# DeltaNet and Fourier mix: a fourth buffer for keys, outputs as pairs of tiles, and the second group's inversion between the steps of the chain

## The chip, the core and the metric

The kernel runs on one NeuronCore of one Trainium2 chip. The metric is the device time of one execution in microseconds (us). The engines are named as the profile names them: PE (TensorE, matmuls), DVE (VectorE), ACT (ScalarE), POOL (GpSimd) and SP (SyncE, which issues DMA transfers here). Each engine works through a list of instructions in a fixed order; an instruction that waits holds up all that stand behind it on its engine.

## What is computed

The inputs q, k, v and beta are float32; the two weight matrices come as 64-bit words, which the kernel turns into float32. The first part is DeltaNet, a recurrence over 768 time steps for 4 batches and 8 heads of dimension 48; the second mixes the result by a real two-dimensional Fourier transform, normalises the rows, and applies a two-layer network.

```python
k_n = k / (np.linalg.norm(k, axis=-1, keepdims=True) + 1e-06)
for t in range(S):                                   # S = 768
    y[:, :, t] = q[t] @ state
    state = state + beta[t] * outer(k_n[t], v[t] - k_n[t] @ state)
x = y as (4, 768, 384)
u = x + real(fft(fft(x, axis=1), axis=2))
un = (u - mean(u)) / sqrt(var(u) + 1e-06)            # over the last axis
out = u + relu(un @ w_ch1) @ w_ch2                   # 384 -> 1536 -> 384
```

## The kernel before, in words

**Chunks, quads, groups.** Time is cut into chunks of 64 steps, 12 for each batch. All 8 heads of a chunk are worked on together. Four chunks make a quad Q (12 in all, three for each batch), two quads a group g (6 in all). The chain runs over the 48 chunks m = 0 to 47, one after the other, because each needs the state that the last one left; chunks 12, 24 and 36 begin a new batch and so a new state.

**Ahead of the chain**, for each quad, `prepare` (L343) transposes keys and queries on PE (tiles `pt`), copies them to the tile `KQT` on ACT (L383 to L388), multiplies keys by keys and by queries (`pg`), copies the products of keys to a triangular system `A` (L414 on DVE, L416 on ACT) and masks those with the queries into `LQ` on DVE (L419). Called for keys alone or queries alone, it does half of this: `keys` and `queries` (L828, L834) do so for the first four quads.

For each group, `invert` (L451) solves the triangular systems of two quads on DVE: a transpose of `A` into `X` (L457), the norms (L428 to L449), a loop of 30 turns with a product (L472) and a sum (L474) each, a product into `Y` (L477), and two transposes into `Z` (L481) and back to `A` (L483). The same function then puts each quad's two 32-wide halves together, in two steps of matmuls (`pj`, L501) and four copies on ACT each (L505 to L509), into the tile `wt`. The second group's `A` lies in `w2`, the space that the second layer's weights fill later; the turns write their products back into `A`.

**A chain step** `chain(m)` (L534): the product of keys and state (`pc<-st`), a difference on DVE (L569, `U` in the first batch and `R` later), in later batches one more product with `wt` (`pc<-R,wt`) and a copy on ACT (L582), the product for the new state (`pc<-U,kp`), and the sum into the other state tile (L599). `outputs` (L605) adds the step's output into `py`, and ACT copies it (L619). In the first batch, `combined` (L514) folds `wt` into keys and values beforehand (`pm`, `pv`). `scaled` (L190) multiplies a quad's values by the lengths of its keys on DVE (L195).

**Beside the chain** go the weights and the second part of the reference. `weights` (L255) loads 64-bit words in slots and turns each piece of 384 columns to float32 by two instructions on ACT (L295, L297) and three on DVE (L311, L314, L317); part 0 is the first layer's `w1`, part 1 is `w2`, with three slots that lie in an output buffer. `fourier(b)` (L646) makes sums and differences of a batch's tiles (L660 and below, tile `scr`), multiplies them with tables (`pf`, `pb`) and adds the result (L696); `mlp` (L733) normalises (`un`, L742), transposes, and runs the two layers (`ph`, `po`).

**What sets the order.** The driver at the end (L839 to L893) steps through generators. At each yield of a chain step it advances `pre` (the preparation and inversion of the group to come) by 2.4 steps and, from step 8 on, `side` (weights, Fourier, network) by 2.4 steps too; before step 8 `side` gets only what `pre` has left over. This gives the program order. A scheduler then places each engine's instructions, with the buffers' releases as limits; what `tc.keep_in_program_order` encloses stays behind all that was traced before it on its engine. `NB` counts the buffers of `KQT`, `LQ` and `wt`.

Of the kernel before, what the change touches and what calls it, by code (L numbers as in the profile page):

```python
# [17 lines left out]
CH = 64  # L18
# [64 lines left out]
def kernel(  # L83
# [23 lines left out]
    NB = 3  # L107
# [15 lines left out]
    def mm(o, lhsT, rhs, start, stop=True):  # L123
        nc.tensor.matmul(o, lhsT=lhsT, rhs=rhs, start=start, stop=stop, skip_group_check=True)  # L124
# [24 lines left out]

    kps = [zeroed([128, QT, 4, 64], f"kp{i}", nc.vector, pads) for i in range(NB + 1)]  # L150
    qps = [zeroed([128, QT, 4, 64], f"qp{i}", nc.vector, pads) for i in range(2)]
    wts = [zeroed([128, QT, 4, CH], f"wt{i}", nc.gpsimd) for i in range(NB)]
# [93 lines left out]
    xbufs = [const.tile([128, NC, DM], F32, name=f"x{i}") for i in range(3)]  # L246
# [8 lines left out]
    def weights(part):  # L255
# [14 lines left out]
        if part == 0:  # L270
            halves = [(w1v[:, i, a * nw:a * nw + nw], w1[:, i, a * nw:a * nw + nw])
                      for i in range(KD) for a in range(2)]
            n, stage = 2, wk.tile([128, 2, nw, 2], I32, tag="hT", name="w64")
        else:
            halves = [(w2v[:, i, a * np_:a * np_ + np_], w2[:, i, a * np_:a * np_ + np_])
                      for i in range(KF) for a in range(DM // np_)]
            n, stage = 1, xbufs[2].rearrange("p t d -> p (t d)")[:, 0:6 * np_].bitcast(I32).rearrange(
                "p (i f two) -> p i f two", i=3, two=2)
        ns = stage.shape[1]

        def fetched(i):
            if i < len(halves):
                nc.sync.dma_start(out=stage[:, i % ns], in_=halves[i][0])

        def words(p):
            i, cs = p // n % ns, slice(p % n * np_, (p % n + 1) * np_)
            return stage[:, i, cs, 0], stage[:, i, cs, 1], tmps[p % 2]
# [12 lines left out]
        for i in range(ns):  # L300
            fetched(i)
        yield
        tmps = [wk.tile([128, 2, np_], I32, tag=tag, name="wtmp") for tag in ("F", "scr")]
        first(0)
        for p in range(n * len(halves)):
# [13 lines left out]
            if (p + 1) % n == 0:  # L319
                fetched(p // n + ns)  # L320
# [8 lines left out]
    def squares(Q):  # L329
# [5 lines left out]
        if Q < 4:  # L335
            Ksq = xbufs[1].rearrange("p t d -> p (t d)")[:, Q % 2 * QT * 4 * D:(Q % 2 + 1) * QT * 4 * D]
            Ksq = Ksq.rearrange("p (n d) -> p n d", d=D)
        else:
            Ksq = wk.tile([128, QT * 4, D], F32, tag="Y", name="Ksq")
# [3 lines left out]
    def prepare(Q, parts=(0, 1)):  # L343
# [5 lines left out]
        again = Q == NB and parts == (1,)  # L349
        taken = (0, 1) if again else parts  # L350
        g, lh = divmod(Q, 2)
        if 0 in parts:
# [7 lines left out]
            if Q == NB:  # L360
                KQT = w2.rearrange("p c m -> p (c m)")[:, 2048:2048 + QT * 8 * CH].rearrange(
                    "p (c j h a t) -> p c j h a t", c=QT, j=2, h=2, a=2)
        if Q != NB and 0 in parts or again:
            KQT = wk.tile([128, QT, 2, 2, 2, CH], F32, tag="KQT", bufs=NB, name="KQT")
        if 0 in parts or again:
# [5 lines left out]
        for c2 in range(QT // 2):  # L371
            for c in (2 * c2, 2 * c2 + 1):
                nt, at0 = len(taken), taken[0]
                pt = ps_one([128, nt, 2, 2, CH], "pt")
                for a in taken:
                    for j in range(2):
                        tr(pt[:, a - at0, j].rearrange("p h t -> p (h t)"),
                           (kp, qp)[a][:, c, 2 * j:2 * j + 2, :].rearrange("p u d -> p (u d)"),
                           a == at0 and j == 0)
                dst = KQT[:, c, :, :, at0:at0 + nt].rearrange("p j h a t -> p a (j h) t")  # L380
# [3 lines left out]
                else:  # L384

                    if nt == 2:
                        nc.scalar.activation(dst[:, 0], src[:, 0], ACT.Copy)
                    nc.scalar.activation(dst[:, nt - 1], src[:, nt - 1, :, ::-1], ACT.Copy)  # L388
# [62 lines left out]
    def invert(g):  # L451
# [3 lines left out]
        A = grams.pop(g)  # L455
        X = wk.tile([128, W, W], F32, tag="X", name="X")
        nc.vector.transpose(X.rearrange("p s t -> p (s t)"),  # L457
                            A[:, :, :, 0].rearrange("p c u s -> p s (c u)"))
# [10 lines left out]
        for j in range(1, W - 1):  # L469
            n = W - 1 - j  # L470
            t = A.rearrange("p c u sl s -> p (c u) sl s")[:, 0:j, 0, 0:n]
            nc.vector.tensor_tensor(t, X[:, j:j + 1, j + 1:].broadcast_to([128, j, n]),  # L472
                                    X[:, 0:j, j:j + 1].broadcast_to([128, j, n]), op=ALU.mult)
# [450 lines left out]
```

## Time and profile before

| | us |
|---|---|
| median of 14 runs | 828.78 |
| lowest and highest of them | 820.47, 840.18 |
| the profiled execution, its time | 831.21 |
| its span, first to last instruction | 829.5 |

The profile has one execution. Its page gives busy times of each engine, the span cut in 40 slices, and groups of instructions. Its other views are a timeline of one engine (start, duration, engine, line, operation, output<-inputs, and in brackets how long the engine had been idle and what ended that), a table of busy times by stretches of the span, groups of instructions within a stretch, and waits added up by what was waited for. Most fp32 matmuls leave more than one record, so counts in the trace are above those of the program. The lines that count are quoted in the prediction.

### The profile page before, as it was taken

The numbers are of one execution on the slowest core, as the hardware profiler recorded it, in microseconds if no ns is written. First come the engines' busy times: TensorE is split into PE (matmuls) and PEld (weight loads), VectorE is DVE, ScalarE is ACT, GpSimd is POOL, SyncE is SP. The second block draws the span as 40 slices with busy tenths as digits, with TensorE's granted clock in tenths as the row PEclk, the third lists the DMA queues.
The fourth block names the chain that finished last, engine by engine and source line by source line (L and its number), as shares of the span: only waits on it lengthen the run. The fifth ranks groups of instructions, "written<-read, shape, count | busy, mean of one in ns | idle before, by whom it ended". The sixth has DMA issues, their size and how long they took to land.

```text
span 829.5 us, 19211 instructions
## 1 busy us (share of the span) xinstructions
PE 738.0 (89%) x8224; PEld 549.5 (66%) x8224; DVE 396.7 (48%) x1036; ACT 290.0 (35%) x679; POOL 45.7 (6%) x67
## 2 busy tenths in 40 slices
PE   3637958996989997889999999999899989999997
PEld 3426857775758765665766766766667667676784
DVE  5885868559964137981169313499110125210000
ACT  3826348253545142371431632511521113030120
POOL 3000000101000000010000001000000010000000
PEclk9999966596997997999999699999699999999999
DMA  7442225212510121101101001001000000000000
GB/s 154 102 111 70 47 40 157 48 29 66 135 40 12 29 49 26 20 13 36 32 17 44 3 10 30 2 1 39 2 6 15 1 20 1 10 9 20 10 9 20
DMA packets 84149, 30.84 MB, mean 37 GB/s; under 512 B 79344, under 2 KB 80880, under 8 KB 84064
## 3 DMA queue, kind: packets, MB, share of 16 engines
q1 hardware_dynamic: 80976, 26.63, 14.4%
q0 software_dynamic: 912, 2.59, 0.9%
q8 instruction: 65, 1.06, 0.5%
q10 hardware_dynamic: 2176, 0.39, 0.3%
q14 instruction: 20, 0.16, 0.1%
HBM read 24.87 MB, written 4.72 MB: 36 GB/s over the span
## 4 chain that ended last, share of the span: by engine, by line
PE 68%; DVE 13%; ACT 11%; DMA 3%; issue 3%; SPq 1%; POOL 0%; POOLq 0%; ACTq 0%; DVEq 0%
PE po L124 20%; PE ph L124 20%; PE py L124 6%; PE pc L124 5%; PE pg L124 3%; PE pj L124 3%; PE pf L124 3%; DVE X L474 2%; PE pt L127 2%; DVE A L472 2%; PE pb L124 2%; ACT wt L506 2%; ACT A L416 2%; DMA x<-in_moe_w_ch_dram 1%; ACT wt L509 1%
## 5 line engine op out<-in xcount | busy, mean ns | idle before, releaser
L124 PE MATMUL ph<-unT,w 128*128 128x256 f32 x864 | 222.6, 405 | 6.2 <-ACT hT L759 2.9
L124 PE MATMUL po<-w,hT 128*128 128x384 f32 x576 | 199.2, 494 | 0.0
L124 PEld LDWEIGHTS ph<-unT,w 128*128 128x128 f32 x864 | 163.0, 198 | 37.1 <-ACT hT L759 6.2
L124 PEld LDWEIGHTS po<-w,hT 128*128 128x128 f32 x576 | 105.3, 190 | 65.8 <-issue 0.3
L759 ACT ACTIVATE hT<-ph 128x256 f32<-128x256 f32 x144 | 54.8, 384 | 185.8 <-PE ph L124 185.4
L599 DVE TENSOR_TENSOR st<-st,pc 48x192 f32<-48x192 f32 x88 | 30.8, 350 | 88.6 <-PE pc L124 62.2
L772 DVE TENSOR_TENSOR x<-x,po 128x384 f32<-128x384 f32 x24 | 13.3, 554 | 120.2 <-PE po L124 120.1
L472 DVE TENSOR_TENSOR A<-X 128x30 f32<-128x30 f32 (+9 forms) x150 | 50.3, 335 | 3.5
L124 PE MATMUL py<-st,KQT 128*64 128x96 f32 x384 | 49.8, 278 | 2.2 <-ACT x L619 2.1
L474 DVE TENSOR_TENSOR X<-X,A 128x30 f32<-128x30 f32 (+9 forms) x150 | 49.4, 329 | 3.4
L582 ACT ACTIVATE U<-pc 128x192 f32<-128x192 f32 x36 | 11.9, 331 | 111.5 <-PE pc L124 96.5
L124 PE MATMUL pg<-KQT 48*64 48x128 f32 (+1 forms) x960 | 36.7, 302 | 13.7 <-ACT KQT L383 13.0
L124 PEld LDWEIGHTS py<-st,KQT 128*64 128x64 f32 x384 | 38.4, 153 | 9.4 <-ACT x L619 4.1
L416 ACT ACTIVATE A<-pg 32x256 f32<-32x256 f32 x108 | 36.7, 369 | 20.4 <-PE pg L124 18.3
L124 PEld LDWEIGHTS pg<-KQT 48*64 48x64 f32 x960 | 29.1, 175 | 21.9 <-ACT KQT L383 16.3
L124 PE MATMUL py<-U,LQ 64*64 64x48 f32 x768 | 42.8, 240 | 0.0
L124 PEld LDWEIGHTS pc<-R,wt 64*64 64x64 f32 x576 | 23.4, 145 | 23.8 <-issue 8.8
L124 PE MATMUL pc<-R,wt 64*64 64x48 f32 x576 | 29.5, 235 | 10.7 <-DVE R L569 6.7
L124 PEld LDWEIGHTS py<-U,LQ 64*64 64x64 f32 x768 | 35.6, 152 | 3.9 <-issue 2.7
L696 DVE TENSOR_TENSOR x<-x,pb 128x193 f32<-128x193 f32 (+1 forms) x96 | 27.1, 344 | 18.4 <-PE pb L124 18.3
L639 POOL DMA_INDIRECT out_dram<-x,rows_hi x12 | 12.2, 1013 | 414.7 <-DVE x L772 198.2
L124 PE MATMUL pf<-stab,scr 128*128 128x128 f32 (+6 forms) x192 | 27.4, 292 | 8.5 <-DVE scr L670 8.3
(133 smaller groups left out, 860.4 us busy)
## 6 DMA issues: line engine op xcount, KB each, us to landing
w<-in_moe_w_ch_dram SPq DMA_DIRECT2D x6, 768.0 KB, 5.0
qp<-in_q_dram SPq DMA_DIRECT2D x96, 48.0 KB, 2.4
V<-in_v_dram SPq DMA_DIRECT2D x96, 48.0 KB, 2.4
x<-in_moe_w_ch_dram SPq DMA_DIRECT2D x12, 384.0 KB, 3.6
kp<-in_k_dram SPq DMA_DIRECT2D x88, 48.0 KB, 2.4
out_dram<-x SPq DMA_DIRECT2D x8, 192.0 KB, 1.9
out_dram<-x SPq DMA_DIRECT2D x4, 168.0 KB, 2.1
stab<-k_stab SPq DMA_DIRECT2D x1, 640.5 KB
```

Source lines behind the costliest of these rows:

```text
L124: nc.tensor.matmul(o, lhsT=lhsT, rhs=rhs, start=start, stop=stop, skip_group_check=True)
L127: nc.tensor.matmul(o, lhsT=src, rhs=ident[0:src.shape[0], 0:src.shape[0]], is_transpose=True, start=start, stop=True, skip_group_check=True)
L416: nc.scalar.activation(ce(A[pr, ns, :, sl]), src, ACT.Copy)
L472: nc.vector.tensor_tensor(t, X[:, j:j + 1, j + 1:].broadcast_to([128, j, n]), X[:, 0:j, j:j + 1].broadcast_to([128, j, n]), op=ALU.mult)
L474: nc.vector.tensor_tensor(X[:, 0:j, j + 1:], X[:, 0:j, j + 1:], t, op=ALU.add)
L506: nc.scalar.activation(wt[r1, :, :, 0:W], Z[r1, ns], ACT.Copy)
L582: nc.scalar.activation(U, pu, ACT.Copy)
L599: nc.vector.tensor_tensor(nst[pr, :, :, e, :], st[pr, :, :, e, :], pS[pr], op=ALU.add)
L639: nc.gpsimd.indirect_dma_start(out=out.rearrange("b s m -> (b s) m"), out_offset=bass.IndirectOffsetOnAxis(ap=rows_hi[:, i:i + 1], axis=0) ...
L696: nc.vector.tensor_tensor(dst, dst, src, op=op)
L759: nc.scalar.activation(hT[:, fc, :], ph, ACT.Relu)
L772: nc.vector.tensor_tensor(x[:, T, :], x[:, T, :], po, op=ALU.add)
```

## The change

- `NB` is 4 for `KQT` and `LQ`; `wt` keeps three buffers (`NW`). There were four buffers for loaded keys and there still are; loaded queries have one buffer instead of two. The fourth quad's keys, which had been transposed into space of `w2` and transposed once more later, go straight to the fourth `KQT`: 8 transposes on PE are gone.
- The three output buffers of six tiles become seven tiles of two, one for each pair that the Fourier mix joins (`xpairs`, `OF_BATCH`).
- `weights(0)` starts after the first loads of keys, queries and values. None of its pieces stands ahead of the first inversion any longer. `w2` is loaded through two slots instead of three (one pair tile and a tile under the tag `scr`).
- For the first two quads, 4 of 6 copies into `A` are on DVE, where 3 of 6 were.
- `invert` ends with the transposes; the rest is `merge`. For the first group, `merge` is called for the first quad alone ahead of the chain and for the second quad within it. The second group's `X` lies in `w2`, and its loop is held in program order. The first matmul of each `pj` is held in program order too.
- Group 2's inversion is not started before `fourier(0)` has been put into the program, and `fourier(0)` is put there as a whole.
- In `fourier`, one sum of 128x1152 (L660) becomes three of 128x384, and its second stage writes to the tile `F`.

```diff
-    NB = 3
+    NB, NW = 4, 3
-    qps = [... for i in range(2)]
-    wts = [... for i in range(NB)]
+    qps = [... for i in range(1)]
+    wts = [... for i in range(NW)]
-    xbufs = [const.tile([128, NC, DM], F32, name=f"x{i}") for i in range(3)]
+    xpairs = [const.tile([128, 2, DM], F32, name=f"x{i}") for i in range(2 * TH + 1)]
+    OF_BATCH = [(0, 1, 2), (3, 4, 5), (0, 1, 6), (3, 4, 2)]
...
-            n, stage = 1, xbufs[2]...   # three slots
+            n, stages = 1, [xpairs[6]...]
+        if part == 1:
+            stages.append(wk.tile([128, np_, 2], I32, tag="scr", name="w64"))
+            fetched(1)
-                fetched(p // n + ns)
+                fetched(p // n + 2)
...
-        again = Q == NB and parts == (1,)
-            if Q == NB:
-                KQT = w2...[:, 2048:2048 + QT * 8 * CH]...
-                        if Q < 2 and hh:
+                        if Q < 2 and (hh or sl):
                             nc.vector.tensor_copy(ce(A[pr, ns, :, sl]), src)
...
     def invert(g):
+        pin = tc.keep_in_program_order if g == 1 else lambda ins: ins
+        if g == 1:
+            X = w2...[:, 2048:2048 + W * W]
+        else:
             X = wk.tile([128, W, W], F32, tag="X", name="X")
-            nc.vector.tensor_tensor(t, ...)
-            nc.vector.tensor_tensor(X[:, 0:j, j + 1:], ...)
+            pin(nc.vector.tensor_tensor(t, ...))
+            pin(nc.vector.tensor_tensor(X[:, 0:j, j + 1:], ...))
...
-        for lh in range(2):
+    def merge(g, lhs=(0, 1)):
+        for lh in lhs:
-                            mm(pj[r1, hh, c, u], *ops, c == 0 and u == 0)
+                            ins = mm(pj[r1, hh, c, u], *ops, c == 0 and u == 0)
+                            if n % QT == 0 and u == 0 and hh == 0:
+                                tc.keep_in_program_order(ins)
...
     def ahead(g):
+        while g == 2 and 0 not in mixed:
+            yield
         yield from invert(g)
+        yield from merge(g)
...
-            yield from fourier(b)
+            run(fourier(b))
+            mixed.add(b)
+            yield
...
-    side = weights(0)
-    advance(side)
-    advance(side, 4)
-    load(1, 1)
+    side = weights(0)
+    advance(side)
     run(both(first, seq(keys(2, 3), queries(0, 1))))
+    pre = both(invert(1), queries(2, 3))
+    advance(pre, 2)
+    run(merge(0, (0,)))
     combined(0)
     combined(1)
-    pre = both(invert(1), queries(2, 3))
+    pre = seq(merge(0, (1,)), pre, merge(1))
```

The scheduler's lists show how this moves instructions. On DVE, between the first inversion's end and the second's loop, stood before (`w_114` is the space of `w2`, `V_978` the values of the second quad):

```order
L481 STREAM_TRANSPOSE Z<-Y 128x32x32
L483 STREAM_TRANSPOSE A<-Y 128x32x32
L195 TENSOR_TENSOR V_978<-V_978,ln 128x768
L457 STREAM_TRANSPOSE X<-w_114 128x1024
L462 SCALAR_TENSOR_TENSOR X<-X,bl 128x1024
L472 TENSOR_TENSOR w_114<-X 128x30
L474 TENSOR_TENSOR X<-X,w_114 128x30
```

and now, with the lines of the changed kernel (L575 is the step's difference, L605 the sum into the state, L414 is `LQ`):

```order
L195 TENSOR_TENSOR V_957<-V_957,ln 128x768
L481 STREAM_TRANSPOSE Z<-Y 128x32x32
L483 STREAM_TRANSPOSE A<-Y 128x32x32
L457 STREAM_TRANSPOSE w_112<-w_112 128x1024
L462 SCALAR_TENSOR_TENSOR w_112<-w_112,bl 128x1024
L476 MEMSET w_112 128x32
L562 COPY st_88<-p_820 48x4x48 x2
L575 TENSOR_TENSOR U<-V_321,pc 128x2x2x48
L605 TENSOR_TENSOR st_90<-st_88,pc 48x4x48 x2
L575 TENSOR_TENSOR U<-V_321,pc 128x2x2x48
L414 TENSOR_TENSOR LQ<-pg,pack 128x2x4x64
L472 TENSOR_TENSOR w_112<-w_112 128x30
```

The loop's first turn now stands behind the differences of steps 0 and 1 and behind the third quad's first `LQ`. On PE, from the first group's merges to the first chain step, stood before:

```order
L124 MATMUL pj<-Z,A 32x32 x32
L124 MATMUL pj<-A 32x32 x32
L124 MATMUL pv<-V_337,wt_84 64x48 x2
L124 MATMUL pj<-Z,A 32x32 x32
L124 MATMUL pv<-V_337,wt_84 64x48 x14
L124 MATMUL pj<-A 32x32 x32
L124 MATMUL p_887<-v0m,k_66 48x192 x2
L127 MATMUL pt<-pack,qp_80 128x128 x2
L124 MATMUL pm<-wt_84,kp_72 64x64 x8
L127 MATMUL pt<-pack,qp_80 128x128 x2
L124 MATMUL pv<-V_337,wt_84 64x48 x5
L124 MATMUL pm<-wt_84,kp_72 64x64 x8
```

and now stands, up to the first `LQ`'s matmuls, with pieces of steps 0 and 1 between:

```order
L124 MATMUL pc<-st_88,KQT 64x48 x8
L124 MATMUL pj<-Z,A 32x32 x32
L127 MATMUL pt<-pack,qp_80 128x128 x2
L124 MATMUL pc<-U,kp_72 48x48 x8
L127 MATMUL pt<-pack,qp_80 128x128 x2
L124 MATMUL py<-st_88,KQT 64x96 x2
L124 MATMUL pj<-A 32x32 x32
L127 MATMUL pt<-pack,qp_80 128x128 x2
L124 MATMUL pc<-st_90,KQT 64x48 x8
```

The first quad's two `pj`, 24 `pv`, 16 `pm` and `p` stand ahead of these rows; the second quad's merge has gone behind step 0, and 16 `pg` for `LQ` follow behind step 1. On DVE, the fourth group's inversion (g = 3) began before like this:

```order
L569 TENSOR_TENSOR R<-V_2913,pc 128x2x2x48
L772 TENSOR_TENSOR x_131<-x_131,po 128x384
L419 TENSOR_TENSOR LQ<-pg,pack 128x2x4x64
L599 TENSOR_TENSOR st_90<-st_92,pc 48x4x48 x2
L457 STREAM_TRANSPOSE X<-A 128x1024
L419 TENSOR_TENSOR LQ<-pg,pack 128x2x4x64
L462 SCALAR_TENSOR_TENSOR X<-X,bl 128x1024
```

and begins now like this:

```order
L575 TENSOR_TENSOR R<-V_2342,pc 128x2x2x48
L414 TENSOR_TENSOR LQ<-pg,pack 128x2x4x64
L605 TENSOR_TENSOR st_88<-st_90,pc 48x4x48 x2
L457 STREAM_TRANSPOSE X<-A 128x1024
L414 TENSOR_TENSOR LQ<-pg,pack 128x2x4x64
L575 TENSOR_TENSOR R<-V_2342,pc 128x2x2x48
L462 SCALAR_TENSOR_TENSOR X<-X,bl 128x1024
```

The transpose stood behind the difference of step 21 and stands behind that of step 17 now, so that the loop falls into the network's stretch and not into the next Fourier mix. In the same way PE's lists put the merges of groups 3, 4 and 5 just before steps 23, 31 and 39, where they stood behind steps 24, 32 and 40.

More of the change, by code (lines that the diff above doesn't have):

```diff
@@ L273, in weights @@
             n, stage = 2, wk.tile([128, 2, nw, 2], I32, tag="hT", name="w64")
+            stages = [stage[:, i] for i in range(2)]
         else:
@@ L298, in first @@
                 t[:, 1].bitcast(F32), hi.bitcast(F32), ACT.Abs, scale=2.0 ** -112))
-        for i in range(ns):
+        for i in range(len(stages)):
             fetched(i)
         yield
-        tmps = [wk.tile([128, 2, np_], I32, tag=tag, name="wtmp") for tag in ("F", "scr")]
+        if part == 1:
+            stages.append(wk.tile([128, np_, 2], I32, tag="scr", name="w64"))
+            fetched(1)
+        tmps = wk.tile([128, 2, 2, np_], I32, tag="F", name="wtmp")
         first(0)
@@ L372, in prepare @@
             for c in (2 * c2, 2 * c2 + 1):
[L373 to L375 removed]
+                pt = ps_one([128, na, 2, 2, CH], "pt")
+                for a in parts:
                     for j in range(2):
[L377 removed]
+                        tr(pt[:, a - a0, j].rearrange("p h t -> p (h t)"),
                            (kp, qp)[a][:, c, 2 * j:2 * j + 2, :].rearrange("p u d -> p (u d)"),
[L379 to L380 removed]
+                           a == a0 and j == 0)
+                dst = KQT[:, c, :, :, a0:a0 + na].rearrange("p j h a t -> p a (j h) t")
                 src = pt.rearrange("p a j h t -> p a (j h) t")
```

102 lines of the change are left out of this document (49 added, 53 removed).

## The prediction

> **What bounds the kernel now.** I read the page first, then busy times by stretches of the span, then the timelines of DVE and PE at the stretches' borders. The page:
>
> ```profile
> span 829.5 us, 19211 instructions
> PE 738.0 (89%) x8224; PEld 549.5 (66%) x8224; DVE 396.7 (48%) x1036; ACT 290.0 (35%) x679; POOL 45.7 (6%) x67
> ```
>
> PE is busy for 89% of the span. Little can be gained where it is full; what the change can move is where PE is not full or runs at a low clock. The stretches (start and end, length, then busy us and records of PE, PEld, DVE, ACT, POOL, the clock granted, the DMA share and GB/s):
>
> ```profile
> core 0: us, PE busy (x) PEld busy (x) DVE busy (x) ACT busy (x) POOL busy (x), PEclk, DMA share, GB/s
> 80.00:116.00 36.00, 29.52 (x702) 25.26 (x700) 30.68 (x84) 10.45 (x26) 0.00 (x0) 0.93 0.30 54
> 116.00:139.00 23.00, 20.22 (x483) 18.40 (x484) 13.69 (x28) 20.13 (x41) 0.00 (x0) 0.52 0.43 124
> 139.00:160.00 21.00, 18.77 (x324) 15.12 (x321) 12.58 (x35) 10.32 (x29) 1.27 (x1) 0.64 0.28 50
> 160.00:197.00 37.00, 29.17 (x322) 23.02 (x321) 26.38 (x73) 12.18 (x32) 4.17 (x8) 0.78 0.15 27
> 197.00:241.00 44.00, 42.87 (x272) 30.61 (x272) 40.06 (x109) 20.66 (x48) 0.73 (x1) 0.93 0.42 108
> 252.00:308.00 56.00, 56.00 (x727) 41.26 (x721) 14.78 (x38) 20.43 (x55) 2.28 (x2) 0.92 0.17 33
> 308.00:372.00 64.00, 51.51 (x741) 40.74 (x740) 54.20 (x151) 27.18 (x60) 4.91 (x7) 0.92 0.10 18
> 372.00:600.00 228.00, 219.31 (x2391) 158.00 (x2384) 110.15 (x280) 77.87 (x183) 10.70 (x15) 0.94 0.09 20
> ...
> 308.00:330.00 22.00, 14.83 (x170) 11.94 (x170) 18.74 (x48) 3.48 (x9) 1.62 (x2) 0.77 0.13 24
> ```
>
> Two stretches matter. From 80 to 116 the second group's inversion runs on DVE (30.68 of 36 us) and step 7 waits for it; from 308 to 372 the second Fourier mix and the fourth group's inversion share DVE (54.20 of 64), and PE is idle for 12.5 us. Between them, from 252 to 308, DVE has 14.78 us of work in 56 while PE is full.
>
> **The change, part by part.** Sums go against the profiled execution (831.21 us, 2.4 above the median of 828.78); the difference is then applied to the median.
>
> *The chain's start.* PE's rows (start, duration) before, around the first two steps:
>
> ```profile
> 71.20 1.92 PE L124 MATMUL pj<-Z,A 32*32 32x32 f32 x64
> 74.91 1.92 PE L124 MATMUL pj<-A 32*32 32x32 f32 x64
> 77.56 0.69 PE L127 MATMUL pt<-pack,qp 128*128 128x128 f32 x2
> 80.39 0.32 PE L124 MATMUL pc<-st,KQT 48*64 48x48 f32 x3
> 85.56 1.13 PE L124 MATMUL pg<-KQT 48*64 48x64 f32 x32
> 86.47 0.62 PE L124 MATMUL pc<-st,KQT 48*64 48x48 f32 x16
> ```
>
> The second quad's two `pj`, 3.8 us, leave the way of step 0, and so do 4 `pt` (two take 0.69): step 0 starts at some 75.3 instead of 80.4. That gains nothing by itself, because step 7 stands behind the second group's merges in both orders. The conversions, `X` and 128x768 value scaling around the first `Z` shift by a microsecond each way; I count nothing there.
>
> *The second inversion starts later.* DVE's rows:
>
> ```profile
> 61.58 2.02 DVE L481 STREAM_TRANSPOSE Z<-Y 128x1024 f32<-128x1024 f32 x1
> 76.46 0.19 DVE L472 TENSOR_TENSOR w<-X 128x30 f32<-128x30 f32 x1
> 86.76 0.69 DVE L419 TENSOR_TENSOR LQ<-pg,pack 128x512 f32<-128x512 f32 x1 [0.56 <-PE pg L124]
> 113.97 1.98 DVE L481 STREAM_TRANSPOSE Z<-Y 128x1024 f32<-128x1024 f32 x1
> 127.69 0.35 DVE L569 TENSOR_TENSOR U<-V,pc 128x192 f32<-128x192 f32 x1
> 158.47 0.35 DVE L569 TENSOR_TENSOR R<-V,pc 128x192 f32<-128x192 f32 x1 [1.95 <-PE pc L124]
> 165.63 0.35 DVE L569 TENSOR_TENSOR R<-V,pc 128x192 f32<-128x192 f32 x1
> ```
>
> The first turn ran at 76.46, at once behind `X`. Now step 1's difference and the third quad's first `LQ` stand ahead of it, and that `LQ` waits on PE for step 1. Steps 0 to 1 took 6.1 us (80.39 to 86.47); with the two `pj` between them and two times 32 records of `pg` (1.13 each; I take 2.1) out, step 1 is at 75.3 + 6.1 + 3.8 - 2.1 = 83.1, and its `pm`, `pv` and the 16 `pg` put `LQ`'s end near 87.4. From the first turn to the `Z` it took 37.5 us; a weight piece (1.5), a copy, two differences, a state sum, an `LQ` and two waits for `pg` (together 4.7) are no longer inside, so `Z` starts near 87.4 + 37.5 - 6.2 = 118.7 and ends near 120.7, 4.7 us later than at 115.95. Without the wait it would have ended earlier, so the added wait is behind PE's step 1: what is queued behind it on DVE is the whole loop.
>
> *Steps 7 to 12.* One `pj` of 1.9 us less stands ahead of step 7, so its difference moves by about 1.5 to 3 us. Then ACT decides:
>
> ```profile
> L295 ACT ACTIVATE wtmp<-w 128x384 int32<-128x384 uint32 x9 | 5.0, 554 | 0.0
> L416 ACT ACTIVATE A<-pg 32x256 f32<-32x256 f32 x12 | 4.1, 369 | 2.5 <-PE pg L124 2.4
> ```
>
> From 116 to 160 ACT had 20.13 + 10.32 = 30.5 us of work, 9 of the 12 conversions of the first layer and one quad's copies among it. All 12 are now there (3 more, at 2 x 0.55 each: 3.3), and the sixth quad's preparation too: at least the 4.1 us of its copies into `A`, at most the 12.18 us of ACT in the stretch 160 to 197; I take 8. That makes 41.8 us behind a `Z` at 120.7, so step 12 (158.47 before) comes no earlier than 162.5. Were all of it added in full, it would come at 158.5 + 4.7 + 11.3 = 174.5. I take 168, in the middle: ACT was idle for 14 of 44 us, and some of that idleness is filled.
>
> *The first Fourier mix.* It took from 160 to 197. The third group's `X` (1.9), its scaling (1.2) and an `LQ` (0.69) leave DVE's queue there; with 26.38 of 37 us busy I count 2.5 of these 3.8. So the network starts at 168 + 36 = 204 where it started at 197: **+7**, from +5 to +9.
>
> *The third group's inversion*, beside the second layer's weights, ended at 240.8:
>
> ```profile
> 206.89 0.55 DVE L311 SCALAR_TENSOR_TENSOR wtmp<-x,wtmp 128x384 int32<-128x384 int32 x1
> 207.36 0.35 DVE L314 TENSOR_SCALAR wtmp<-wtmp 128x384 int32<-128x384 int32 x1
> 207.87 0.55 DVE L317 CUSTOM_DVE_ANT_0 w<-wtmp 128x768 uint16<-128x768 uint16 x1
> 212.45 0.55 DVE L311 SCALAR_TENSOR_TENSOR wtmp<-x,wtmp 128x384 int32<-128x384 int32 x1
> 238.86 1.97 DVE L481 STREAM_TRANSPOSE Z<-Y 128x1024 f32<-128x1024 f32 x1
> ...
> x<-in_moe_w_ch_dram SPq DMA_DIRECT2D x12, 384.0 KB, 3.6
> ```
>
> The two rows of L311 are three pieces apart: 5.56 us is one turn of a slot, made of the load (3.6), two ACT instructions (1.1) and this one. With three slots a piece takes 1.85 us, with two 2.8. Twelve pieces then need 5 turns, 27.8 us, for 3 turns, 16.7. Not all of these 11 us count, since turns of the loop stand between the pieces in both orders: with two pieces at 1.45 (0.55, 0.35, 0.55) and some five loop instructions at 0.35 to 0.4, DVE has about 4.7 us of work in each 5.56. I get two ends: bound by DVE's work alone, and with four turns (2.3 us) done ahead, +7 - 2.3 = +4.7; bound by the loads, 206.5 + 27.8 + 3 for the last pieces + 9.7 for the rest of the loop, `Y` and `Z` = 247, +6.2. I take **+5.5**, from +2.7 (network at +5) to +8.2 (at +9).
>
> *Steps 17 to 24.* The fourth group's preparation and inversion now come early, into a full PE and an idle DVE. The network's work is used up earlier, and steps 20 to 23 have hardly any beside them. The nearest rows are those of steps 22 and 23 and what PE did between:
>
> ```profile
> 310.81 0.35 DVE L569 TENSOR_TENSOR R<-V,pc 128x192 f32<-128x192 f32 x1
> 316.18 0.35 DVE L569 TENSOR_TENSOR R<-V,pc 128x192 f32<-128x192 f32 x1 [1.22 <-PE pc L124]
> ...
> 311.81 0.69 PE L127 MATMUL ptr<-pack,un 128*128 128x128 f32 x3
> 313.78 1.96 PE L124 MATMUL ph<-unT,w 128*128 128x256 f32 x4
> ```
>
> The step took 5.37 us, 2.65 of it network work. Without that, three such steps leave 8 us of PE idle, less the two `pj` (3.8) that stand there now: **+4**. If the steps last as long as from 12 to 13 (7.16 us, rows above), it is 3 x 4.4 - 3.8 = +9.4; if `pj` and preparation cover all, 0.
>
> *The second Fourier mix.* DVE's largest group from 308 to 372 is half of the inversion's loop:
>
> ```profile
> L472 DVE TENSOR_TENSOR A<-X 128x30 f32<-128x30 f32 (+14 forms) x30 | 10.9, 364 | 0.5
> ```
>
> The other half (L474) is as many sums, so some 21 of the 54.20 us are the loop, and some 8 more its transposes and products. They go to where DVE was idle. PE's 12.5 us of idleness should then fall to what a mix without an inversion shows: from 372 to 600 PE is idle for 3.8% of the time, 2.5 us in 64; I leave 3, so 9.5 are gained, and 1.5 for the clock, which was 0.77 from 308 to 330 (at 14.83 us of PE work, 3.4 at most). **-11**; from -14 to -6, if only the first 22 us, 7.2 of them idle, lose 4.5 and 1.5.
>
> *The last two merges* stand a step earlier on PE; what they waited for from 372 to 600:
>
> ```profile
> PE pc L124 <- ACT wt L508: 3.2, 2, 2.0
> PE pj L124 <- DVE Z L481: 1.5, 2, 1.1
> ```
>
> At most 4.7 is saved, at least nothing: **-2**. The eight transposes less and three sums for one in `fourier` are below 1 us each way, beside full engines.
>
> **Sum:** +5.5 + 4 - 11 - 2 = -3.5 us. 831.2 becomes 827.7, and the median 828.8 becomes **825.3**.
>
> **The rivals.**
>
> *Full relief.* The fourth buffer takes the inversions out of PE's way and the starved steps are covered: +2.7 + 0 - 14 - 4.7 = -16, 812.8 us. For it: DVE's 14.78 of 56 us from 252 to 308. Against it: PE is full there, so that work taken in early pushes other work out.
>
> *No effect that can be told.* The second mix waits for its own sums, not for the inversion, and loses only 6 us of its idleness: 5.5 + 4 - 6 - 2 = +1.5, 830.3. For it: 7.2 of the 12.5 us lie in the first 22 us, where the mix makes its first sums.
>
> *Slower: steps 20 to 23 starve.* Each step is as long as its chain of waits over PE, DVE and ACT when nothing else is there. At 7.16 us a step, +9.4, and with a gain of only 6 behind it: 5.5 + 9.4 - 6 - 0 = +8.9, 837.7. It decides from about 6 us a step on. Against it: 5.37 us was seen with the clock low.
>
> *The clock.* From 116 to 139 PE is busy for 20.22 of 23 us, and the granted clock is 0.52. If the clock came back there, PE's 29.17 us of the first mix, at 0.78, could shrink by 3 to 6, and the time would be 822. The Trainium skill, in "TensorE: Matmul & The Clock Gate", Part 1, says that the full rate returns after about 3.4 us of sustained work. By that rule the 23 us at 0.52 could not be; the trace disagrees, so it has a small chance.
>
> **How the numbers follow.** Forecast 0.38 (821 to 830); relief 0.20; no effect 0.17; starving 0.20; clock 0.05. About 0.5% is what a measurement of this kernel can tell from no change: below 824.6 is faster, above 832.9 slower. Faster: 0.17 of the forecast, 0.20 and 0.04, 0.41. Same: 0.19, 0.12 and 0.01, 0.32. Slower: 0.02, 0.05 and 0.20, 0.27. The range has the bounds of the unknown terms, with relief and starving less 1 in 10 at either end: 811 to 840.
>
> **What would show it.** Right: the second loop's first turn near 87 and `Z` near 121; step 12 near 168; weight pieces of `w2` 2.8 us apart; the fourth group's turns between steps 18 and 22; PE idle near steps 21 to 23 and little in the second mix. Wrong: a turn of the loop ahead of the third quad's `LQ`; step 12 before 163; pieces 1.9 us apart; or PE idle for 10 us or more in the second mix, which would mean that DVE was not what it waited for.

## The result, and the profile after

The changed kernel takes 808.9 us (median of 10 runs, 805.6 to 814.5) against 829.4 us (47 runs): a ratio of 0.9787, with a 95% interval from 0.9754 to 0.982. The forecast was 825.3; its range from 811 to 840 holds 0.9787 x 828.78 = 811.1 only at its very edge, which is luck: the lower bound came from the terms of full relief, and those are not what made up the difference (see below). The change is some 2% faster, where I had expected hardly anything.

The pages' first lines, after the change, with the slices of the granted clock, which the prediction did not show for the kernel before:

```profile
span 805.0 us, 19238 instructions
PE 717.8 (89%) x8216; PEld 534.0 (66%) x8216; DVE 400.6 (50%) x1055; ACT 288.3 (36%) x675; POOL 47.5 (6%) x67
PEclk9999985879999998699999999999999999999999
```

and before:

```profile
PEclk9999966596997997999999699999699999999999
```

PE's share is 89% in both, but its busy time fell by 20.2 us, with 8 records less of 8224. A matmul that takes longer counts as busier, and the two low digits of the clock beyond slice 20 (6 in slices 23 and 29) are gone. What the clock does to a matmul shows in `pj` of the same 64 records, from two merges of the kernel before, the first at full clock and the second at half:

```profile
352.98 1.20 PE L124 MATMUL pj<-Z,A 32*32 32x32 f32 x64
462.89 1.92 PE L124 MATMUL pj<-Z,A 32*32 32x32 f32 x64 [0.17 <-ACT wt L508]
```

I cut both spans at the same two places of the program: the difference on DVE of step 24 and that of step 41. The columns are those of the prediction's table of stretches. After:

```profile
0.00:328.60 328.60, 255.99 (x4160) 199.03 (x4162) 231.09 (x597) 157.22 (x362) 21.13 (x31) 0.90 0.30 70
328.60:576.62 248.02, 243.05 (x2777) 178.38 (x2775) 134.09 (x361) 91.33 (x217) 16.03 (x22) 0.99 0.10 22
576.62:805.00 228.38, 218.73 (x1286) 156.61 (x1285) 35.41 (x98) 39.70 (x97) 10.31 (x14) 0.99 0.03 11
```

Before:

```profile
0.00:318.60 318.60, 257.39 (x3970) 201.23 (x3971) 206.37 (x538) 148.07 (x347) 19.79 (x31) 0.88 0.32 71
318.60:598.74 280.14, 261.06 (x2993) 191.25 (x2989) 155.43 (x406) 102.54 (x236) 15.61 (x22) 0.95 0.09 20
598.74:829.50 230.76, 219.53 (x1270) 157.03 (x1270) 34.94 (x94) 39.35 (x96) 10.31 (x14) 0.98 0.03 11
```

Step 24 comes 10.0 us later. From there to step 41 it is 32.1 us less, and behind it 2.4 less: 24.5 in all (these two executions lie a little further apart than the medians). In the middle stretch, idle time of PE fell from 19.1 to 5.0 us, and the clock rose from 0.95 to 0.99, which is 14.0 and 2.5 us of full clock lost. Some work moved out of this stretch to the first one: group 3's first three `pj`, which took 1.20 us each there, 3.6 in all, and nine records of `ph`, some 2.3 us:

```profile
L124 PE MATMUL ph<-unT,w 128*128 128x256 f32 x327 | 91.3, 417 | 4.1 <-ACT hT L759 2.0 <-ACT KQT L388 0.7 <-ACT gz L693 0.6
L124 PE MATMUL ph<-unT,w 128*128 128x256 f32 x318 | 80.2, 392 | 2.4 <-ACT hT L765 1.0 <-ACT KQT L383 0.9 <-ACT F L697 0.2
```

So 32.1 is 14.1 of idleness, some 11.5 of clock (a clock of two digits leaves 1 to 2 us open), 5.9 of moved work, and 0.6 that I did not take apart.

Cut further, at steps 27 and 36, the middle stretch gave 6.7, 9.8 and 15.6 us. Before:

```profile
318.60:383.20 64.60, 54.22 (x710) 41.14 (x707) 48.61 (x135) 27.90 (x62) 5.83 (x9) 0.95 0.10 18
383.20:509.00 125.80, 121.97 (x1337) 86.91 (x1336) 50.86 (x126) 42.47 (x99) 4.30 (x4) 0.95 0.11 25
509.00:598.70 89.70, 84.83 (x950) 63.16 (x949) 55.95 (x146) 32.17 (x75) 5.47 (x9) 0.94 0.06 13
```

After:

```profile
328.60:386.50 57.90, 55.58 (x596) 42.81 (x594) 37.53 (x111) 23.51 (x60) 5.74 (x9) 0.94 0.10 18
386.50:502.50 116.00, 114.99 (x1333) 81.34 (x1332) 55.51 (x136) 42.37 (x103) 4.62 (x4) 1.00 0.12 26
502.50:576.60 74.10, 72.45 (x852) 54.21 (x853) 41.05 (x115) 25.45 (x54) 5.67 (x9) 1.00 0.08 18
```

In the first of the three, which holds the second mix, PE's idle time fell by 8.1 us and its clock did not rise. The other 25.4 us came in the two later ones, with the last two groups' merges: 6.0 of idle time and nearly all of the clock. In the stretch ahead of step 24 idle time rose by 11.4 us, from 61.2 to 72.6.

PE's waits within the middle stretch (in total, times, longest), the largest at the mix and the merges before, and then the two largest after:

```profile
PE pf L124 <- DVE scr L670: 5.2, 2, 4.5
PE pc L124 <- ACT wt L508: 3.4, 3, 2.0
PE pj L124 <- ACT A L505: 2.3, 3, 0.9
PE pj L124 <- DVE Z L481: 1.5, 2, 1.1
```

```profile
PE pf L124 <- DVE scr L676: 1.2, 1, 1.2
PE py L124 <- ACT x L625: 1.0, 2, 0.6
```

The waits at the merges of groups 4 and 5 have gone altogether. Group 3's merge stands ahead of step 24 now and still waits there, 2.1 us for its `Z` and 0.5 for ACT. The second mix's longest wait has gone from 4.5 to 1.2.

### The profile page after: what moved, and what is told of

It is laid out like the page before. It is cut to its first block, busy times and chain, and to the rows that moved or that the text cites. A ratio compares the mean times of both kernels' runs of the same rounds, so it can differ in the third digit from the quotient of the medians.

```text
span 805.0 us, 19238 instructions
## 1 busy us (share of the span) xinstructions
PE 717.8 (89%) x8216; PEld 534.0 (66%) x8216; DVE 400.6 (50%) x1055; ACT 288.3 (36%) x675; POOL 47.5 (6%) x67
## 4 chain that ended last, share of the span: by engine, by line
PE 47%; DVE 5%; ACT 2%; issue 1%; DMA 1%; POOL 0%; POOLq 0%; SPq 0%; DVEq 0%; ACTq 0%
PE ph L124 19%; PE po L124 16%; PE py L124 3%; PE pc L124 3%; PE pb L124 2%; PE pf L124 2%; DVE X L474 1%; DVE A L472 1%; PE pj L124 1%; PE ptr L127 1%; PE pg L124 1%; ACT A L411 1%; PE pt L127 0%; ACT hT L765 0%; POOL F L669 0%
## 5 line engine op out<-in xcount | busy, mean ns | idle before, releaser
L124 PE MATMUL ph<-unT,w 128*128 128x256 f32 x864 | 210.6, 391 | 5.8 <-ACT hT L765 3.1
L124 PEld LDWEIGHTS ph<-unT,w 128*128 128x128 f32 x864 | 158.8, 191 | 36.8 <-ACT hT L765 7.5
L765 ACT ACTIVATE hT<-ph 128x256 f32<-128x256 f32 x144 | 55.0, 383 | 170.6 <-PE ph L124 170.3
L605 DVE TENSOR_TENSOR st<-st,pc 48x192 f32<-48x192 f32 x88 | 30.7, 349 | 56.3 <-PE pc L124 39.5
L124 PE MATMUL pg<-KQT 48*64 48x64 f32 (+1 forms) x1024 | 40.1, 302 | 14.6 <-ACT KQT L378 13.9
L124 PEld LDWEIGHTS pg<-KQT 48*64 48x64 f32 x1024 | 31.7, 176 | 25.6 <-ACT KQT L378 18.3
L411 ACT ACTIVATE A<-pg 32x256 f32<-32x256 f32 x104 | 35.6, 370 | 18.5 <-PE pg L124 16.8
L124 PEld LDWEIGHTS py<-st,KQT 128*64 128x64 f32 x384 | 36.1, 146 | 8.9 <-ACT x L625 3.9
L124 PE MATMUL py<-U,LQ 64*64 64x48 f32 x768 | 40.1, 228 | 0.0
L414 DVE TENSOR_TENSOR LQ<-pg,pack 128x512 f32<-128x512 f32 x24 | 16.5, 689 | 40.3 <-ACT A L411 35.1
L124 PEld LDWEIGHTS py<-U,LQ 64*64 64x64 f32 x768 | 33.2, 141 | 2.7 <-issue 1.1
L625 ACT ACTIVATE x<-py 64x384 f32<-64x384 f32 x44 | 21.3, 483 | 36.9 <-PE py L124 35.5
L127 PE MATMUL pt<-pack,kp 128*128 128x128 f32 x96 | 22.9, 342 | 7.8 <-DMA pack<-k_pack 4.2
```

Source lines behind the costliest of these rows:

```text
L124: return nc.tensor.matmul(o, lhsT=lhsT, rhs=rhs, start=start, stop=stop, skip_group_check=True)
L127: nc.tensor.matmul(o, lhsT=src, rhs=ident[0:src.shape[0], 0:src.shape[0]], is_transpose=True, start=start, stop=True, skip_group_check=True)
L411: nc.scalar.activation(ce(A[pr, ns, :, sl]), src, ACT.Copy)
L414: nc.vector.tensor_tensor(ce(LQ[:, 2 * c2:2 * c2 + 2]), pv[:, :, :, 1 - a0], mb[:, None, None, :].broadcast_to([128, 2, 4, CH]), op=ALU.mult)
L605: nc.vector.tensor_tensor(nst[pr, :, :, e, :], st[pr, :, :, e, :], pS[pr], op=ALU.add)
L625: nc.scalar.activation(xs[b][T % TH][yr, T // TH].rearrange("p (h u d) -> p h u d", h=2, u=4), py[yr], ACT.Copy, scale=live[yr] if n == NC ...
```

## The experiments

Two questions: what part of the change brings this, and is it idle time or the clock? In the table, the last columns are the time of the difference of step 24, the stretch from step 24 to 41, and the stretch behind it, each from one profile in us.

| kernel | ratio to before (95%) | step 24 | 24 to 41 | behind |
|---|---|---|---|---|
| before | 1 | 318.6 | 280.1 | 230.8 |
| changed | 0.9787 (0.9754 to 0.982) | 328.6 | 248.0 | 228.4 |
| changed, late preparation | 1.0281 (1.0179 to 1.0383) | 328.0 | 289.3 | 226.8 |
| changed, last group late | 0.986 (0.9793 to 0.9927) | 328.8 | 260.8 | 226.5 |
| changed, merge whole | 0.9786 (0.969 to 0.9883) | 329.6 | 247.9 | 228.4 |
| changed, no hold | 0.9764 (0.969 to 0.9839) | 331.0 | 251.3 | 228.4 |
| storage alone, first time | 0.9683 (0.9616 to 0.9751) | 325.5 | 250.7 | 228.4 |
| storage alone, again | 0.9649 (0.9572 to 0.9726) | 319.9 | 252.6 | 228.4 |
| storage, with the hold | 0.9732 (0.9634 to 0.9831) | 317.5 | 251.4 | 228.4 |
| storage, late preparation | 1.005 (1.0007 to 1.0093) | 316.3 | 286.1 | 226.3 |
| before, three sums | 1.0007 (0.9961 to 1.0053) | 316.7 | 289.3 | 226.8 |
| before, filler | 1.0278 (1.0158 to 1.0398) | 315.9 | 305.3 | 229.3 |

**Late preparation in the changed kernel.** Through this condition the fourth buffer sets the order from the third group on:

```diff
     def ahead(g):
         for Q in (2 * g, 2 * g + 1):
-            while Q >= NB and Q - NB in held:
+            while Q >= 3 and Q - 3 in held:
                 yield
             squares(Q)
```

> The changed kernel, with one condition put back: each quad from the fifth on is prepared only when the quad three before it has left the chain, as with three buffers. The merges of groups 3, 4 and 5 then stand behind steps 24, 32 and 40 again, as before the change; the rest stays changed. Theory A (the time went with spells of half clock that follow the waits around the merges): the spells at the fifth and sixth group's merges, 13 and 14 us of half clock, come back, the clock falls from 0.954 to about 0.94, and the time rises from 809 by 11 to 14 us to 820 to 823, ratio to before 0.990. Rival B (the gain is from the early part and the Fourier mixes, not from the fourth buffer): no change from 809, ratio 0.979.

Measured: 850.2 us, ratio 1.0281, slower even than the kernel before. Theory A's direction held and its size did not: 41 us, not 11 to 14. Rival B is out. Step 24 comes when it came in the changed kernel; all that is lost is lost behind it:

```profile
328.03:617.29 289.26, 271.54 (x2993) 199.47 (x2989) 155.00 (x411) 102.38 (x236) 15.57 (x22) 0.91 0.10 20
```

Idle 17.7 us instead of 5.0, and a clock of 0.91 instead of 0.99.

**The last group late.** The same condition for group 5 alone:

```diff
-            while Q >= NB and Q - NB in held:
+            while Q - (3 if g == 5 else NB) in held:
```

> The changed kernel, with the late condition of three buffers for the last group alone. Theory A (each late group costs its own waits and the spell of half clock behind them): from step 36 to step 41 the profile gets 13 to 16 us longer, from 74 to 87 to 90, the time 809 rises to 820 to 825, ratio 0.990 to 0.994. Rival G (one late group is made up for by the full PE of the stretch behind it): 809 to 813, ratio 0.978 to 0.982.

Measured: 817.0 us, ratio 0.986; from step 36 to 41 it took 90.2 us instead of 74.1:

```profile
499.31:589.51 90.20, 84.76 (x950) 63.28 (x949) 55.36 (x149) 32.27 (x75) 5.46 (x9) 0.95 0.06 13
```

The stretch did what theory A said; the total rose by 8.1 us by the medians and by 11.0 between the two profiled executions, between the two expectations. In the profiles the other 5 us came back outside the stretch: step 36 came 3.2 us earlier, and the end behind step 41 is 1.9 shorter. Most likely that is the preparation that moved into this stretch and left an earlier one.

**Filler in the kernel before.**

```diff
+                if g >= 4:
+                    fill = ps_one([128, 256], "fill")
+                    for k in range(2):
+                        tc.keep_in_program_order(nc.tensor.matmul(fill,
+                            lhsT=w1[:, 0, 0:128], rhs=stab[:, 0:256], start=True, ...))
                 yield
```

> The kernel before, with two more matmuls of 128x128 by 128x256 behind each of the four pj of groups 4 and 5: 16 in all, some 8.8 us of PE work that nothing reads. Theory A: they fill most of the waits at these merges, the two spells of half clock behind them (13 and 14 us) do not come, 13 us are saved and 4 to 9 paid: 5 to 9 us faster than before, ratio 0.990 to 0.994, clock about 0.943 where it was 0.929. Rival C (the clock falls whatever stands there, or its loss is only a picture of idle time): 4 to 9 us slower, ratio 1.005 to 1.011.

Measured: 852.8 us, ratio 1.0278. Neither: it did not fill the wait. Held in program order, the filler kept the network's matmuls from passing it, and the `pj` that had waited 0.4 us for its `Z` waited 6.8:

```profile
591.17 1.92 PE L124 MATMUL pj<-Z,A 32*32 32x32 f32 x64 [6.81 <-DVE Z L481]
```

In the kernel before, a `ph` of 3.19 us stood ahead of that `pj`; here nothing stands in the gap. This says nothing for or against the clock, only that what PE has beside a merge is what hides it.

**Three sums in the kernel before.**

```diff
-            nc.vector.tensor_tensor(eo, lo, hi, op=op)
+            for T in range(TH):
+                nc.vector.tensor_tensor(eo[:, T], lo[:, T], hi[:, T], op=op)
```

> The kernel before, with the first sum of each Fourier mix (128x1152) cut into three of 128x384, nothing else. Theory A: in the last mix PE's wait of 2.3 us becomes 1.5, as in the changed kernel, and the spell of half clock behind it, about 10 us, goes: 4 to 5 us faster, ratio 0.994 to 0.995. Rival C: each mix gains at most the 0.8 us of its wait or loses the 0.2 us that two more instructions cost: ratio 0.998 to 1.001.

Measured: ratio 1.0007. Rival C's range holds, and theory A's 0.994 to 0.995 lies outside the interval (0.9961 to 1.0053). The wait in the last mix fell from 2.29 to 1.48 us as expected, and the stretch behind step 41 is 4 us shorter, but 9 more are lost between steps 24 and 41 in that execution. Its middle stretch has 17.7 us of idle time, against 19.1 in the kernel before, so the 9 are not idle time; its granted clock there is 0.91, against 0.95. Which spells of low clock an execution has is not the same in these two, so one that is gone is no sure gain.

**The first merge whole.**

```diff
-    run(merge(0, (0,)))
+    run(merge(0))
...
-    pre = seq(merge(0, (1,)), pre, merge(1))
+    pre = seq(pre, merge(1))
```

> The changed kernel with the first group's merge put whole ahead of the chain again, so that step 0 starts some 4 us later. Prediction's theory (step 7 waits for the second group's merges whatever step 0 does): no change from 809 within 0.3%, ratio 0.977 to 0.981. Rival D (the earlier start of the chain counts): 4 us slower, ratio 0.984.

Measured: 809.5 us, ratio 0.9786. The earlier start of the chain is worth nothing that can be told, as predicted, but not for the reason given: step 7 did not stand still, it came at 135.3 us instead of 131.2, and the delay was made up by step 12 (171.9 instead of 170.6). Rival D's 0.984 is within the interval, but step 24 and the stretches behind it are those of the changed kernel within 1 us.

**One wait in a full PE.** In the changed kernel, within the last batch, a matmul is made to wait for a short chain on DVE (4 sums, or 14 in the second kernel):

```diff
-                    mm(po, ...)
+                    ins = mm(po, ...)
+                    if b == B - 1 and i == 1 and tt == 1 and fc == 0:
+                        tc.keep_in_program_order(ins)
...
+                if b == B - 1 and i == 1 and tt == 0:
+                    late = wk.tile([128, 4 * D], F32, tag="R", name="late")
+                    nc.vector.tensor_copy(late, po[:, 0:4 * D])
+                    for _ in range(4):
+                        nc.vector.tensor_tensor(late, late, late, op=ALU.add)
+                    ps_late = ps_one([128, 4 * D], "ps_late")
+                    tc.keep_in_program_order(mm(ps_late, ident, late, True))
```

> The changed kernel with one wait put into PE's last stretch, where it is full and at full clock: behind the first po of the last batch's second pair a matmul waits for a copy and four sums on DVE, some 2.3 us. It adds work that nothing reads. Theory A (a short wait is followed by a spell of half clock): a spell of 10 us or more behind it, the stretch longer by 2.3 + 5 us or more. Rival C (the wait is paid once): longer by 2.3 us, clock 1.00 behind it.

> The same with fourteen sums, a wait of some 5.5 us. Theory A: a spell of half clock of 12 us or more, the stretch longer by 5.5 + 6 us or more. Rival C: longer by 5.5 us.

Measured, one execution each: 812.0 and 817.9 us. The stretch behind step 41 took 233.2 and 237.1 us, 4.9 and 8.7 more than in the changed kernel. PE's timeline with the short and then with the long wait:

```profile
764.08 0.80 PE L124 MATMUL ps_late<-late,pack 128*128 128x192 f32 x2 [2.58 <-DVE late L786]
764.67 9.40 PE L124 MATMUL po<-w,hT 128*128 128x384 f32 x24
```

```profile
770.34 0.98 PE L124 MATMUL ps_late<-late,pack 128*128 128x192 f32 x2 [6.51 <-DVE late L786]
771.11 9.14 PE L124 MATMUL po<-w,hT 128*128 128x384 f32 x24
755.82 8.01 PE L124 MATMUL po<-w,hT 128*128 128x384 f32 x24
```

The 24 records that take 8.01 us without a wait take 9.40 and 9.14 behind one: 1.1 to 1.4 us more, not 5 or 6. With the wait itself and the added matmul (0.80 and 0.98) that is all but 0.1 of the 4.9 and 8.7. Theory A is wrong for dense work, though rival C is not quite right either. The granted clock of the four microseconds behind the short wait, and of two microseconds behind the long one, each as a stretch of its own:

```profile
764.00:768.00 4.00, 3.92 (x8) 2.48 (x9) 0.00 (x0) 0.00 (x0) 0.00 (x0) 0.57 0.01 4
772.00:774.00 2.00, 2.00 (x5) 0.99 (x5) 0.00 (x0) 0.00 (x0) 0.00 (x0) 0.60 0.00 0
```

It was 1.00 in the next stretch of both, so the low clock lasted some 3.5 us behind the wait. Behind a merge in the kernel before it lasted from about 462 to 476, with PE busy for 13.55 of these 14 us; there PE ran this (the first rows of it):

```profile
462.28 0.45 PE L124 MATMUL pc<-R,wt 64*64 64x48 f32 x2 [1.18 <-ACT wt L508]
462.89 1.92 PE L124 MATMUL pj<-Z,A 32*32 32x32 f32 x64 [0.17 <-ACT wt L508]
464.74 1.08 PE L124 MATMUL pc<-R,wt 64*64 64x48 f32 x14
...
467.76 1.92 PE L124 MATMUL pj<-A 32*32 32x32 f32 x64
469.61 0.57 PE L124 MATMUL pc<-U,kp 64*48 64x48 f32 x16
```

Matmuls of 32 and 64 rows stand between those of 128. That these keep the clock low for longer is a guess, which no run tried by itself. They do not lower it alone: the same kernel's merge from 353 to 364 ran at a clock of 1.00, with `pj` of 1.20 us.

**The storage alone.** The changed kernel's storage with the order of before, that is the fourth buffer, the pairs of output tiles, the two slots, the eight transposes less and the three sums, without the change's reordering: first layer's weights early, first merge whole, no `keep_in_program_order` on `pj` and on the loop, `X` of the second group in its old place, the mix spread, no hold, and copies into `A` as before.

```diff
-        pin = tc.keep_in_program_order if g == 1 else lambda ins: ins
-        if g == 1:
-            X = w2...
+        pin = lambda ins: ins
...
-                            if n % QT == 0 and u == 0 and hh == 0:
-                                tc.keep_in_program_order(ins)
...
-        while g == 2 and 0 not in mixed:
-            yield
...
-            run(fourier(b))
-            mixed.add(b)
-            yield
+            yield from fourier(b)
...
+    side = weights(0)
+    advance(side)
     run(keys(0))
...
+    advance(side, 4)
...
-    run(merge(0, (0,)))
+    run(merge(0))
     combined(0)
     combined(1)
-    pre = seq(merge(0, (1,)), pre, merge(1))
+    pre = both(seq(invert(1), merge(1)), queries(2, 3))
```

> The changed kernel's storage (four buffers for keys, pairs of output tiles, two slots for the second layer's weights) with the order of before: first layer's weights early, the first group's merge whole ahead of the chain, no matmul and no loop held in program order, the second group's X in its old place, the Fourier mix spread and not waited for. Theory E (the fourth buffer alone carries the gain; the changed order costs the 9 us by which step 24 came later): 795 to 803, ratio 0.957 to 0.967. Rival F (the order is needed, since the early preparation would otherwise be starved or late in the first 24 steps): 809 to 820, ratio 0.975 to 0.988.

> The changed storage with the order of before once more, in more rounds, to set it against the changed kernel's 0.9787 with its interval from 0.9754 to 0.982. If the changed order costs some 5 us: ratio 0.966 to 0.973, its interval's upper end below 0.9787. If the first run was luck: 0.975 to 0.982.

Measured: 802.9 us (ratio 0.9683, 0.9616 to 0.9751), and again 803.8 us (0.9649, 0.9572 to 0.9726). It beats both kernels: both intervals end below the changed kernel's 0.9754 to 0.982, the first only just, and the second puts rival F out. Theory E holds at its upper end, its range of ratios missed by 0.001 the first time; but the changed order costs some 5 us, not the 9 of which it spoke. The middle stretch of the second run:

```profile
319.90:572.48 252.58, 247.02 (x2786) 181.52 (x2787) 133.48 (x353) 91.74 (x219) 15.88 (x22) 0.98 0.11 22
```

Step 24 stands 1.3 us behind the kernel before in this execution and 6.9 in the first one, not 10, and the gain behind it is nearly that of the changed kernel.

**The storage with late preparation.** The condition of the first experiment, in the storage-alone kernel:

> The changed storage with the order of before (803 us) and the late condition of three buffers for groups 2 to 5. Theory A (preparing a group's second quad four steps earlier is what the fourth buffer brings; pairs of tiles, two weight slots and the eight transposes less bring next to nothing): back at the time before, 826 to 832, ratio 0.996 to 1.004. Rival H (the storage itself, without the earlier preparation, brings a good part): 810 to 822, ratio 0.977 to 0.99.

Measured: 832.3 us, ratio 1.005 (1.0007 to 1.0093). Back at the time before or a little above; rival H is out. The pairs of tiles, the two slots, the eight transposes less and the three sums together bring nothing without the earlier preparation. The steadiest sign is PE's idle time from step 24 to 41: it is 16.8 to 19.1 us in the kernel before, the same with three sums and the two with late preparation of all groups, and 4.7 to 6.6 in the six traces with early preparation of all groups.

```profile
316.31:602.38 286.07, 269.32 (x2993) 197.54 (x2989) 155.20 (x412) 102.36 (x236) 15.57 (x22) 0.92 0.10 21
```

**The hold**, put into the storage-alone kernel and taken out of the changed one (the lines on `mixed`, and `run(fourier(b))` or `yield from fourier(b)`):

> The changed storage with the order of before (803 us), and only the hold put in: the third group's inversion starts when the first Fourier mix is in the program, and that mix goes there as a whole. If the hold is what the changed order costs: 807 to 811, ratio 0.973 to 0.978. If the early part is (second loop behind the first LQ, first layer's weights later): 801 to 805, ratio 0.966 to 0.970.

> The changed kernel with the hold alone taken out: the third group's inversion does not wait for the first Fourier mix, and that mix is spread over the steps. If the hold is what the changed order costs: 801 to 805, ratio 0.966 to 0.970. If the early part is: 807 to 811, ratio 0.973 to 0.978.

Measured: 804.1 us, ratio 0.9732 (0.9634 to 0.9831), and 809.4 us, ratio 0.9764 (0.969 to 0.9839). By their medians both stay with the early part that they have, not with the hold, though the first one's ratio, by its own runs of the kernel before, is at the edge of the other expectation; the intervals overlap, so this is likely and not shown. The traces point the same way: step 24 stands at 328.0 to 331.0 in the five kernels of the table with the changed early part, hold or not, and at 317.5 to 325.5 in those with the fourth buffer and the old one. What in the early part costs the 5 us (the loop's order, the weights' place, the copies) was not taken apart.

## Why the forecast was too high

- *What bounds it, and where the change acts:* right in kind, by the early preparation that the fourth buffer allows, and wrong in place. I looked for 11 us in the second mix and 2 in the last merges; the stretch with the mix gave 6.7 and the two behind it 25.4. With the other order that preparation brings 803.8 instead of 832.3, with the changed order 808.9 instead of 850.2.
- *The second inversion starts later, and steps 7 to 12:* near in each number. The first turn at 87.7 (forecast 87.4), `Z` from 119.9 to 121.9 (120.7), step 12 at 170.6 (168):

```profile
87.70 0.18 DVE L472 TENSOR_TENSOR w<-w 128x30 f32<-128x30 f32 x1
119.87 2.01 DVE L481 STREAM_TRANSPOSE Z<-Y 128x1024 f32<-128x1024 f32 x1
121.90:170.60 48.70, 37.09 (x844) 30.90 (x844) 33.22 (x76) 40.28 (x95) 1.27 (x1) 0.74 0.41 104
```

  ACT's work between them is 40.3 us, for which I had 41.8.
- *The first Fourier mix:* from the difference of step 12 to the first `un` it took 29.1 us instead of 37.6; it lost 8.5 where I counted 2.5. The first `un` came at 199.7, 3.6 us later than before (196.0), not 7.
- *The two weight slots:* wrong. I took a value between DVE's work and the load's turn of 5.56 us; the turns took 4.5 us, with DVE busy for 21.2 of the 22.7 us of five turns, so DVE's work alone set them. From the first piece to the eleventh are five turns:

```profile
202.73 0.56 DVE L315 SCALAR_TENSOR_TENSOR wtmp<-x,wtmp 128x384 int32<-128x384 int32 x1
225.44 0.55 DVE L315 SCALAR_TENSOR_TENSOR wtmp<-x,wtmp 128x384 int32<-128x384 int32 x1
236.85 2.07 DVE L481 STREAM_TRANSPOSE Z<-Y 128x1024 f32<-128x1024 f32 x1
```

  The third group's `Z` ended 1.9 us earlier than before, where I had +5.5.
- *Steps 17 to 24:* step 24 came 10.0 us later, and my two terms gave 9.5, but by the wrong road. PE did not starve; from step 20 to 24 it was idle for 2.7 of 24.3 us. Some 5.9 of the 10 are work that stands ahead of step 24 now and not behind it, three `pj` and nine records of `ph`. I used two `pj` to fill idle time and did not take them off the stretch that they left. Net of this work, the early part cost 4.1 us. PE's idle time ahead of step 24 rose by 11.4 us; between the differences of steps 0 and 12 alone it rose by 13.2.
- *The second mix and the last merges:* idle time fell by 14.1 us where I had 9.5 and 2: by 8.1 in the mix and by 6.0 behind it. My bound of 4.7 for the merges left out two rows of the same view, 1.9 us in all:

```profile
PE pj L124 <- ACT A L505: 1.4, 2, 0.8
PE pj L124 <- ACT wt L508: 0.5, 2, 0.3
```

- *The clock:* **this is the term that was mis-sized most.** I gave it 1.5 us, for the second mix alone, from the one low row that I had quoted, 308 to 330, and did not look at the stretches behind 372, whose mean of 0.94 was in my own table: 6% of 228 us is 13.7 us of clock lost there. In the middle stretch some 11.5 came back, and by the rows above behind the mix, not in it. Over the runs I estimate it at half: the mean clock of 40 runs of the kernel before, taken beside the experiments, is 0.934, of 12 of the changed one 0.951; among runs of one kernel the time falls by 580 to 710 us for each unit of clock, so 0.017 of clock is 10 to 12 us of the 20. No run changed the clock and left the waits as they were, so that the clock is a cost of its own, beside the waits, rests on this and on the `pj` of 1.20 and 1.92 us.
- *The rivals:* full relief (812.8, given 0.20) came nearest, by luck in the number: it had 14 us for the mix, with the clock there, and the mix's stretch gave 6.7; it had 4.7 for the merges, and the stretches behind gave 25.4, half of it by the clock, for which it had nothing there. Starving did not come. The clock rival named the mechanism for another stretch, and with the wrong reason. The rule that I cited from the Trainium skill, "TensorE: Matmul & The Clock Gate", Part 1, is borne out by the two runs with a wait in dense work (some 3.5 us at low clock behind the wait). From 116 to 139 and behind two merges (462 to 476 and 589 to 602 us) the low clock lasted far longer, so there the trace does not bear it out.

Summed as the forecast was: 4.1 lost in the early part net of moved work (9.5 foreseen), and gained 14.1 of idle time (11.5 foreseen), some 11.5 of clock (1.5), 2.4 behind step 41 (0), and 0.6 that is open: 24.5 in these two executions. The 2.4 are not the fourth buffer's: the kernel before with three sums has 4.0 less there.

## What to carry to other kernels

A buffer that lets a stage run one unit earlier is worth what the stage's waits cost where they fall now, plus the clock that they cost behind them: price it by the idle time and by the share of low clock of all stretches in which they fall, not of the first one. Test a bundle of edits by its conditions: one condition put back showed that the buffer's early preparation carried the whole gain, and that the reordering added with it gave some back.

## What the runs showed of the hardware

- Within one kernel the time varies with the granted clock from run to run: 821.6 us at 0.945 and 836.6 at 0.924 for the kernel before.
- A wait of 2.6 or 6.5 us in dense 128-row matmuls cost 1.1 to 1.4 us of low clock beyond itself. Behind two merges of the kernel before, with 32- and 64-row matmuls between, the clock stayed at half for some 14 us though PE was busy (13.55 of 14.0 us from 462 on).
- A `pj` of 64 records took 1.20 us at full clock and 1.92 at half.
